# Moving input splits into attention and spreading a weight split over five tiles, at the seam of two stages of a fused kernel

## The chip, the cores and the metric

One Trainium2 chip, one core of it. The metric is device time of one execution in microseconds (us). The core has a matrix engine (PE, TensorE), a vector engine (DVE, VectorE), a scalar engine (ACT, ScalarE), GpSimd (POOL) and SP (SyncE), which here issues nearly all DMAs. Each engine works through its own queue in order and waits on semaphores that the others raise.

## The reference

Three layers in a row: pooled attention, a gated layer with a spatial product, a mixture of experts with one expert per token. What matters here is the first layer's end and the second layer:

```
q_pool = q.reshape(B, H, S // 2, 2, D).mean(axis=3)          # B 4, H 8, S 1152, D 64
attn = softmax(q_pool @ k^T / sqrt(D)); attn_out = attn @ v
x = attn_out.transpose(0, 2, 1, 3).reshape(B, 576, 512)
h = np.maximum(x @ w_in, 0.0); u, v = h[..., :512], h[..., 512:]
v_n = (v - mean(v)) / np.sqrt(var(v) + 1e-06)
v_s = np.einsum('ts,bsd->btd', w_spatial, v_n) + b_spatial[None, :, None]
x = (u * v_s) @ w_out                                         # then the experts
```

## The kernel before, in words

**Attention** (`attention`, L30 to L295) works on 16 pairs of heads, nine tiles each: 144 tiles g, t = g mod 9 within pair p. For a tile, PE makes scores (L82 to L98), DVE takes the largest (L105, L112), ACT the exponentials (L123, L125), PE transposes them (L137), DVE and ACT bring the transposes back (L155, L153), and PE multiplies by v (L203) into one accumulator `av`. Row sums are added and inverted on DVE (`sums`, L164, L165: instructions of 4 or 5 columns), turned by PE, stored to DRAM and loaded back broadcast over the partitions (`spread`, L188, L190, tile `rb`); DVE multiplies the accumulator by `rb` (L211, L213, `out`), and SP stores the result `xT` (L214). A table of times sets the order: `at(time, f)` puts a step at a place counted in tiles, and the sorted table is written out engine by engine; no scheduler moves anything. GpSimd sums and scales the next pair's q (`prep`, L71, L72), and 16 jobs round w_in into a high and a low part in the background (`weights_steps`).

All products of the later layers are made of a high part (rounded to the matrix engine's fast float32 form) and a low part (the rest): hi*hi + lo*hi + hi*lo. `split` (L365) makes the two: ACT rounds (L368), DVE or GpSimd subtracts (L372).

**The seam.** `Moe1.begin` (L393) loads batch 0's x when attention's last scores are issued, into the place where u's weights go later; `split_x` (L420) splits it on ACT, DVE and GpSimd beside the last products with v; `begin_x1` (L403) loads batch 1's x; `begin_u` (L407) loads u's weights after the last eviction. v's weights (`begin_v`, L387) come at tile 134.92, 2 MB.

**The gated layer** (`Moe1.rest`, L426) takes two batches at a time. Five v tiles come first (`v_tile`, L512): twelve matmuls, Relu on ACT (L522), statistics on DVE (L524 to L527), and one tile later `norm` (L529): a square root on ACT (L532), DVE's normalization (L533 to L537), vn's high part on DVE (L370) and its low part on GpSimd (L372). The fifth tile's rows go into `vta` and `vtb`, partly by SP's copies (L547). Between the v tiles stand batch 1's splits (L652 to L657). Then three u tiles (`u_tile`, L552), and the first spatial tile (`sp_tile`, L566), which needs vn, w_spatial's two parts (`wsh`, `wsl`) and `wt`, w_spatial's last tile with the bias. w_spatial (1.64 MB, L443) is loaded after the last store of x, and `w_rest` (L584) splits all five of its tiles together behind the second u tile. From there on the w_out conversion (`conv`, forty small steps on DVE and ACT) runs between the spatial tiles.

```
        def w_rest(norm):
            norm()
            for k in range(5):
                w_sp(k)
            bias()
```

## Time and profile before

| | us |
|---|---|
| runs shown | 1066.67, 1064.51, 1060.57; median 1064.51 |
| profiled execution, its own time | 1063.56 |
| its span, first to last instruction | 1061.7 |
| PE busy | 1008.2 (95%) |
| DVE busy | 748.7 (71%) |
| ACT busy | 595.3 (56%) |
| GpSimd busy | 225.5 (21%) |
| chain that ended last | PE 75%, DVE 10%, DMA 7%, issue 4%, ACT 2%, POOL 1% |

The times of the runs are of whole executions; the span leaves out 1.9 us around the instructions. Busy shares are means over stages with different limits: attention lasts to about 510 us of the span, the gated layer to about 750, the experts to the end. In a wait list the engine named first waited, the one behind the arrow ended the wait. In a chain of waits each piece was released by the one above it.

### The profile page before, as it was taken

The page shows a single profiled execution, that of the slowest core. Times are in us where ns is not written, and L with a number is a line of the kernel's source. Part 1 is how long each engine was busy: PE and PEld are TensorE (multiplying, and loading weights), DVE is VectorE, ACT ScalarE, POOL GpSimd, SP SyncE. Part 2 cuts the span into 40 slices and gives each one's busy share as a digit, 9 for nine tenths or more (in the row PEclk, how much of TensorE's full clock was granted, in tenths as well). Part 3 has the DMA queues.
Part 4 walks back from the last instruction along what each step waited for, and adds up shares of the span by engine and source line. Part 5 has one row for each costly group of instructions (what it writes and reads, how often), then busy time and mean ns, then how long its engine had stood idle before and what let it go on. Part 6 is the DMA issues. An engine that isn't in the chain of part 4 may idle for free.

```text
span 1061.7 us, 19763 instructions
## 1 busy us (share of the span) xinstructions
PE 1008.2 (95%) x7532; PEld 679.5 (64%) x7532; DVE 748.7 (71%) x1361; ACT 595.3 (56%) x1172; POOL 225.5 (21%) x189
## 2 busy tenths in 40 slices
PE   6899999999999999999879999999999999999997
PEld 3444444444544444444668988998777777777775
DVE  6787787878777787776498414232688787888884
ACT  4666666666666666666323322122277777777773
POOL 1111111111101111100355312231212321213111
PEclk9999999999999999999979999999999999999999
DMA  4444223443433343331512111001745142112840
GB/s 164 139 132 134 80 86 133 135 135 131 133 87 116 95 136 125 125 120 68 204 56 80 34 65 59 1 1 39 248 181 201 37 148 92 40 41 83 312 176 28
DMA packets 50495, 116.75 MB, mean 110 GB/s; under 512 B 8986, under 2 KB 21586, under 8 KB 48856
## 3 DMA queue, kind: packets, MB, share of 16 engines
q1 hardware_dynamic: 46672, 104.37, 29.0%
q0 software_dynamic: 3680, 11.02, 3.2%
q8 instruction: 62, 1.02, 0.4%
q14 instruction: 41, 0.34, 0.1%
q10 hardware_dynamic: 40, 0.01, 0.0%
HBM read 165.61 MB, written 19.47 MB: 174 GB/s over the span
## 4 chain that ended last, share of the span: by engine, by line
PE 75%; DVE 10%; DMA 7%; issue 4%; ACT 2%; POOL 1%; SPq 0%; POOLq 0%; DVEq 0%; ACTq 0%
PE ps_av L203 15%; PE ps_t L137 11%; PE ep_yp L1074 8%; PE ps_s L82 8%; PE ep_hp L1041 6%; DMA er_x<-x,tab_gi 4%; PE m_ps_v L626 4%; PE m_ps_u L574 4%; PE m_ps_u L560 3%; PE m_ps_v L519 3%; PE ep_hp L1034 3%; PE ps_r L95 3%; DVE aw_mx L105 2%; PE ps_s L85 2%; DMA ao_qr<-in_q 1%
## 5 line engine op out<-in xcount | busy, mean ns | idle before, releaser
L137 PEld LDWEIGHTS ps_t<-keep_ident,aw_e 64*128 64x128 f32 x2592 | 104.0, 140 | 193.1 <-DVE aw_et L155 130.3
L105 DVE TENSOR_REDUCE aw_mx<-ps_s 128x1 f32<-128x1024 f32 x144 | 174.7, 1213 | 8.3 <-ACT aw_e L125 2.5
L155 DVE COPY aw_et<-ps_t 128x640 f32<-128x640 f32 x144 | 118.5, 823 | 81.8 <-PE ps_t L137 81.5
L203 PE MATMUL ps_av<-aw_et,aw_v 128*64 128x320 f32 (+1 forms) x1152 | 168.9, 420 | 0.0
L125 ACT ACTIVATE aw_e<-ps_s,aw_mx 128x1024 f32<-128x1024 f32 x144 | 159.2, 1106 | 0.0
L137 PE MATMUL ps_t<-keep_ident,aw_e 64*128 64x64 f32 x2592 | 143.5, 235 | 15.8 <-DVE aw_et L155 12.0
L82 PE MATMUL ps_s<-ao_k,ao_q 64*128 64x512 f32 x512 | 141.7, 632 | 7.2 <-DMA ao_k<-in_k 6.0
L123 ACT ACTIVATE aw_e<-ps_r,aw_mx 128x128 f32<-128x128 f32 x144 | 53.0, 368 | 130.4 <-DVE aw_junk L112 130.4
L153 ACT ACTIVATE aw_et<-ps_t 128x512 f32<-128x512 f32 x144 | 86.0, 597 | 54.7 <-PE ps_t L137 53.4
L372 DVE TENSOR_TENSOR eb_w2l<-er_r,eb_w2h 128x1024 fp32r<-128x1024 f32 x88 | 103.5, 1217 | 4.2 <-ACT eb_w2h L368 4.1
L203 PEld LDWEIGHTS ps_av<-aw_et,aw_v 128*64 128x64 f32 x1152 | 72.0, 137 | 49.0 <-issue 4.1
L372 DVE TENSOR_TENSOR eb_w1l<-er_r,eb_w1h 128x1024 fp32r<-128x1024 f32 x66 | 78.7, 1221 | 33.6 <-ACT eb_w1h L368 33.6
L368 ACT ACTIVATE eb_w2h<-er_r 128x1024 fp32r<-128x1024 f32 x88 | 88.7, 1068 | 0.6 <-PE ep_yp L1074 0.3
L368 ACT ACTIVATE eb_w1h<-er_r 128x1024 fp32r<-128x1024 f32 x66 | 67.8, 1071 | 17.4 <-DMA er_r<-in_w 13.2
L372 POOL TENSOR_TENSOR bg_l<-bg_e,bg_h 128x256 fp32r<-128x256 f32 x16 | 11.6, 728 | 296.5 <-ACT bg_h L368 296.5
L1074 PE MATMUL ep_yp<-eb_w2h,ew_hth 128*128 128x512 f32 x176 | 71.2, 404 | 0.2 <-ACT ew_hth L368 0.2
L1074 PE MATMUL ep_yp<-eb_w2h,ew_htl 128*128 128x512 f32 x176 | 70.2, 399 | 0.2 <-DVE ew_htl L372 0.2
L1074 PE MATMUL ep_yp<-eb_w2l,ew_hth 128*128 128x512 f32 x176 | 69.1, 392 | 0.0
L1080 POOL DMA_INDIRECT out<-ew_y,tab_si x22 | 22.4, 1017 | 206.8 <-DVE ew_y L1079 183.2
L112 DVE TENSOR_SCALAR_CACHE_REDUCE aw_junk<-ps_r,aw_mx 128x128 f32<-128x128 f32 x144 | 49.9, 346 | 14.4
L71 POOL TENSOR_TENSOR ao_qr<-ao_qr 128x576 f32<-128x576 f32 x30 | 43.2, 1442 | 72.6 <-DMA ao_qr<-in_q 72.1
L95 PE MATMUL ps_r<-ao_k,ao_q 64*128 64x128 f32 x256 | 57.2, 304 | 0.0
(240 smaller groups left out, 1908.5 us busy)
## 6 DMA issues: line engine op xcount, KB each, us to landing
er_r<-in_w SPq DMA_DIRECT2D x45, 2048.0 KB
ao_qr<-in_q SPq DMA_DIRECT2D x32, 576.0 KB
ao_k<-in_k SPq DMA_DIRECT2D x32, 320.0 KB
aw_v<-in_v SPq DMA_DIRECT2D x16, 576.0 KB
xT<-aw_xo SPq DMA_DIRECT2D x16, 288.0 KB
bg_raw<-in_w_in SPq DMA_DIRECT2D x16, 256.0 KB
aw_rb<-rdram SPq DMA_DIRECT2D x64, 64.0 KB
er_r<-in_w SPq DMA_DIRECT2D x16, 256.0 KB
```

Source lines behind the costliest of these rows:

```text
L82: nc.tensor.matmul(d["s"][:, i, :], r["q", h][rows, 128 * n:128 * n + 128], r["k", h][rows, 0:512], start=True, stop=True)
L95: nc.tensor.matmul(d["r"][:, 0:128], r["q", h][rows, 128 * n:128 * n + 128], r["k", h][rows, 512:640], start=True, stop=True)
L105: nc.vector.tensor_reduce(out=m[:, 0:1], in_=d["s"], op=ALU.min, axis=AX.XY)
L125: nc.scalar.activation(out=e[:, 0:8, :].rearrange("p k c -> p (k c)"), in_=d["s"].rearrange("p i c -> p (i c)"), func=AF.Exp, bias=d["m"][ ...
L137: nc.tensor.transpose(t[:, i, 64 * (k - k0):64 * (k - k0) + 64], E[g]["e"][o, k, :], ident[o, o])
L153: nc.scalar.activation(out=o, in_=i, func=AF.Copy)
L155: nc.vector.tensor_copy(o, i)
L203: nc.tensor.matmul(box["t"][64 * h:64 * h + 64, 0:n], v[:, h, k, :], et[:, k, h, 0:n], start=k == 0, stop=k == 8)
L368: nc.scalar.activation(out=hi, in_=src, func=AF.Copy)
L372: (nc.gpsimd if eng_lo == "p" else nc.vector).tensor_tensor(out=lo, in0=src, in1=hi.bitcast(F32), op=ALU.subtract)
L1041: nc.tensor.matmul(pt[c], xT[xi][:, 128 * k:128 * k + 128], W1[wi][:, k, 512 * c:512 * c + 512], start=False, stop=todo[c] == 0)
L1074: nc.tensor.matmul(pt, hT[hi][:, c, 128 * o:128 * o + 128], W2[wi][:, f, :], start=f == 0 and (hi, wi) == (0, 0), stop=f == 7 and (hi, wi) ...
```

## The change

It concerns the seam. x of batches 0 and 1 is loaded at tile 82.3, when both are complete in DRAM, and split on GpSimd alone in eight steps (`begin_split`) at places of the table between tiles 86 and 140: one instruction rounds, one subtracts. The pool of q and k moves to the right side so that x's place on the left is free by then. u's weights are loaded at tile 137.92. In the last eviction DVE copies the accumulator to SBUF and multiplies from the copy. w_spatial's first four tiles are split one by one between the v tiles; the fifth stays where it was.

```diff
@@ -36,7 +36,7 @@
         early = ctx.enter_context(ExitStack())
-        opr = Pool(early.enter_context(tc.tile_pool(name="a_op", bufs=2)), "ao")
+        opr = Pool(early.enter_context(tc.tile_pool(name="a_op", bufs=2, side="right")), "ao")
         ps = Pool(ctx.enter_context(tc.tile_pool(name="a_ps", bufs=1, space=PSUM)), "ps")
@@ -207,6 +207,9 @@
                 xo, rb, t = P[p]["xo"], P[p]["rb", c], box["t"]
+                if p == NP - 1 and c:
+                    t = wrk([128, 320], F32, "av", bufs=1)
+                    nc.vector.tensor_copy(t, box["t"][:, 0:320])
                 m, e = (64, 0) if b % 2 else (0, 512)
@@ -275,11 +278,13 @@
             at(g + 1.11, evac)
-        at(NT - 1 + .3, lambda: (early.close(), hooks["S"]()))
+        at(NT - 1 + .3, early.close)
         at(NT - 10.4, lambda: [bg.pop(0)[1]() for _ in range(len(bg))])
-        at(NT - 9.08, hooks["raw"])
-        at(NT + 1.45, hooks["T"])
-        at(NT + 1.46, hooks["x1"])
+        at(82.3, hooks["x"])
+        for n, slot in enumerate((86, 95, 104, 113, 122, 125, 131, 140)):
+            at(slot + .21, hooks["split"], n)
+        at(NT - 9.08, hooks["v"])
+        at(NT - 6.08, hooks["u"])
         load_qk(0, 0)
@@ -292,7 +297,6 @@
         evac()
-        hooks["end"]()
@@ -395,14 +399,20 @@
         self.xx = [big([128, 4, 2 * SQ], F32R, f"x{i}") for i in "hl"]
-        self.x0 = [raw[h // 3][:, SQ * (h % 3):SQ * (h % 3) + SQ] for h in range(4)]
+        x0 = [raw[h // 3][:, SQ * (h % 3):SQ * (h % 3) + SQ] for h in range(4)]
         self.nc.sync.dma_start(raw[0][:, 0:3 * SQ], self.xT[0, :, 0:3, :])
         self.nc.sync.dma_start(raw[1][:, 0:SQ], self.xT[0, :, 3, :])
-        self.x1 = big([128, 4 * 640], F32, "wsh")[:, 0:4 * SQ].rearrange("p (h c) -> p h c", h=4)
-
-    def begin_x1(self):
-        for c in (slice(0, 64), slice(64, SQ)):
-            self.nc.sync.dma_start(self.x1[:, :, c], self.xT[1, :, :, c])
+        x1 = big([128, 4 * 640], F32, "wsh")[:, 0:4 * SQ].rearrange("p (h c) -> p h c", h=4)
+        self.nc.sync.dma_start(x1, self.xT[1])
+        self.raws = x0 + [x1[:, h, :] for h in range(4)]
+
+    def begin_split(self, n):
+
+        b, h = divmod(n, 4)
+        g, x, c = self.nc.gpsimd, self.raws[n], self.of(b, 0, SQ)
+        hi, lo = (self.xx[i][:, h, c] for i in range(2))
+        g.tensor_scalar(out=hi, in0=x, scalar1=1.0, scalar2=0.0, op0=ALU.mult, op1=ALU.add)
+        g.tensor_tensor(out=lo, in0=x, in1=hi.bitcast(F32), op=ALU.subtract)
@@ -432,6 +442,7 @@
         ps2 = self.ps2 = self.pool(self.right, "m_ps2", 3, space=PSUM)
+        wsh = self.big([128, 4, 640], F32R, "wsh")
         wsl = big([128, 4, 640], F32R, "wsl")
@@ -583,8 +594,7 @@
             norm()
-            for k in range(5):
-                w_sp(k)
+            w_sp(4)
             bias()
@@ -648,13 +658,9 @@
                     norm()
+                    if P == 0:
+                        w_sp(j - 1)
                 norm = n
-                if P == 0 and j == 1:
-                    c = of(1, 0, 64)
-                    split(nc, xx[0][:, :, c], xx[1][:, :, c], self.x1[:, :, 0:64], "a", "v")
-                if P == 0 and j == 2:
-                    split_x(1, [self.x1[:, h, 64:SQ] for h in range(4)], o=64)
-                    wsh = self.big([128, 4, 640], F32R, "wsh")
             norms = []
@@ -1209,8 +1215,8 @@
         bg = weights_steps(nc, Pool(bgp.enter_context(tc.tile_pool(name="bg", bufs=1, side="right")), "bg"), jobs, False)
-        hooks = {"raw": lambda: m1.begin_v(keep([128, 4096], F32R, "wv").rearrange("p (n k c) -> p n k c", n=2, k=4)),
-                 "S": m1.begin, "x1": m1.begin_x1, "T": lambda: m1.split_x(0, m1.x0), "end": m1.begin_u}
+        wv = keep([128, 4096], F32R, "wv").rearrange("p (n k c) -> p n k c", n=2, k=4)
+        hooks = {"x": m1.begin, "split": m1.begin_split, "v": lambda: m1.begin_v(wv), "u": m1.begin_u}
         attention(tc, nc, ap, cst, xT, bg, hooks)
```

The changed kernel's lines from L210 on are numbered higher: 3 more behind the copy (L212), 4 in `split` (L372, L376), 10 or 11 in `rest` (Relu L533, square root L543).

**ACT, over the first four square roots to the first u tiles.** `m_wrk_v` is a v tile's Relu, `m_wrk_mv` a square root, `m_a_xh` x's high part (its source `m_a_wsh` is batch 1's x), `m_a_wsh` as an output w_spatial's high part, `m_wrk_u` a u tile. Before:

```order
L368 ACTIVATE m_a_xh_6553<-m_a_wsh_6557 128x4x64
L522 ACTIVATE m_wrk_v_6785<-m_ps_v_6772 128x512
L532 ACTIVATE m_wrk_mv_6759<-m_wrk_mv_6759 128x1
L368 ACTIVATE m_a_xh_6553<-m_a_wsh_6557 128x512 x4
L522 ACTIVATE m_wrk_v_6822<-m_ps_v_6809 128x512
L532 ACTIVATE m_wrk_mv_6789<-m_wrk_mv_6789 128x1
L522 ACTIVATE m_wrk_v_6850<-m_ps_v_6837 128x512
L532 ACTIVATE m_wrk_mv_6826<-m_wrk_mv_6826 128x1
L564 ACTIVATE m_wrk_u_6890<-m_ps_u_6865 128x576
L564 ACTIVATE m_wrk_u_6917<-m_ps_u_6892 128x576
L532 ACTIVATE m_wrk_mv_6854<-m_wrk_mv_6854 128x1
L368 ACTIVATE m_a_wsh_6808<-m_r_gh_6703 128x640 x4
```

Now:

```order
L543 ACTIVATE m_wrk_mv_6749<-m_wrk_mv_6749 128x1
L372 ACTIVATE m_a_wsh_6708<-m_r_gh_6713 128x640
L533 ACTIVATE m_wrk_v_6795<-m_ps_v_6782 128x512
L543 ACTIVATE m_wrk_mv_6769<-m_wrk_mv_6769 128x1
L372 ACTIVATE m_a_wsh_6708<-m_r_gh_6713 128x640
L533 ACTIVATE m_wrk_v_6825<-m_ps_v_6812 128x512
L543 ACTIVATE m_wrk_mv_6799<-m_wrk_mv_6799 128x1
L372 ACTIVATE m_a_wsh_6708<-m_r_gh_6713 128x640
L533 ACTIVATE m_wrk_v_6855<-m_ps_v_6842 128x512
L543 ACTIVATE m_wrk_mv_6829<-m_wrk_mv_6829 128x1
L372 ACTIVATE m_a_wsh_6708<-m_r_gh_6713 128x640
L575 ACTIVATE m_wrk_u_6897<-m_ps_u_6872 128x576
```

x's rounding has left this stretch (and, ahead of it, batch 0's four), and one rounding of w_spatial stands behind each of the four square roots, the first ahead of the third Relu.

**SP, end of attention.** `aw_row` is the row of inverted sums on its way to DRAM, `aw_rb` the broadcast, `xT<-aw_xo` the last store of x, `m_a_wih` and `m_a_wil` from `xT` batch 0's x and from `wi_d` u's weights, `m_r_gh<-in_w_sp` w_spatial. Before, from the last pair's second row on:

```order
L180 DMA rdram<-aw_row_623_6626 5x128
L405 DMA m_a_wsh_6557<-xT 128x4x64
L405 DMA m_a_wsh_6557<-xT 128x4x512
L188 DMA aw_rb_624_6629<-rdram 64x2x128
L190 DMA aw_rb_624_6629<-rdram 64x64
L188 DMA aw_rb_624_6629<-rdram 64x2x128
L190 DMA aw_rb_624_6629<-rdram 64x64
L214 DMA xT<-aw_xo_6610 128x576
L410 DMA m_a_wih_6667<-wi_d 128x4x512
L410 DMA m_a_wil_6668<-wi_d 128x4x512
L442 DMA m_r_gh_6703<-in_b_sp 2x640 x2
L443 DMA m_r_gh_6703<-in_w_sp 128x5x640
```

Now:

```order
L180 DMA rdram<-aw_row_623_6647 5x128
L188 DMA aw_rb_624_6650<-rdram 64x2x128
L190 DMA aw_rb_624_6650<-rdram 64x64
L188 DMA aw_rb_624_6650<-rdram 64x2x128
L190 DMA aw_rb_624_6650<-rdram 64x64
L217 DMA xT<-aw_xo_6631 128x576
L453 DMA m_r_gh_6713<-in_b_sp 2x640 x2
L454 DMA m_r_gh_6713<-in_w_sp 128x5x640
```

Batch 1's x no longer stands between row and broadcast, nor u's weights between the store and w_spatial.

**GpSimd, pairs 10 to 12 in attention.** `ao_qr` and `ao_q` are the q preparation, `bg_l` the low part of a background job, `m_a_xh` and `m_a_xl` the new splits. Before:

```order
L372 TENSOR_TENSOR bg_l_4264<-bg_e_4066,bg_h_4263 128x256
L71 TENSOR_TENSOR ao_qr_67_4164<-ao_qr_67_4164 128x576
L72 TENSOR_SCALAR ao_q_71_4311<-ao_qr_67_4164 128x576
L71 TENSOR_TENSOR ao_qr_69_4216<-ao_qr_69_4216 128x576
L72 TENSOR_SCALAR ao_q_72_4352<-ao_qr_69_4216 128x576
L372 TENSOR_TENSOR bg_l_4635<-bg_e_4433,bg_h_4634 128x256
```

Now:

```order
L376 TENSOR_TENSOR bg_l_4278<-bg_e_4080,bg_h_4277 128x256
L71 TENSOR_TENSOR ao_qr_67_4178<-ao_qr_67_4178 128x576
L72 TENSOR_SCALAR ao_q_71_4325<-ao_qr_67_4178 128x576
L71 TENSOR_TENSOR ao_qr_69_4230<-ao_qr_69_4230 128x576
L72 TENSOR_SCALAR ao_q_72_4366<-ao_qr_69_4230 128x576
L414 TENSOR_SCALAR m_a_xh_3815<-m_a_wih_3813 128x576
L415 TENSOR_TENSOR m_a_xl_3816<-m_a_wih_3813,m_a_xh_3815 128x576
L376 TENSOR_TENSOR bg_l_4651<-bg_e_4449,bg_h_4650 128x256
```

A split of two instructions follows the second q preparation, ahead of the next background job.

## Rows read from the trace of the kernel before

**Rows 1.** PE time line, 510-552: start us, us, engine, line, op [idle before].
```profile
513.99 0.53 PE L519 MATMUL m_ps_v<-keep_wv,m_a_xh 128*128 128x512 f32 x1 [3.86 <-issue]
...
545.71 0.61 PE L574 MATMUL m_ps_u<-m_b_wsl,m_b_vnh 128*128 128x288 f32 x1 [6.41 <-DVE m_b_wsl L372]
...
549.96 0.61 PE L577 MATMUL m_ps_u<-m_b_wta,m_b_vta 128*128 128x288 f32 x1 [0.59 <-DVE m_b_wta L471]
```

**Rows 2.** Busy us by window: PE, PEld, DVE, ACT, POOL, clock, DMA, GB/s.
```profile
465.00:470.00 5.00, 5.00 (x60) 2.70 (x61) 3.54 (x8) 3.09 (x9) 0.00 (x0) 1.00 0.94 321
515.00:520.00 5.00, 5.00 (x17) 3.96 (x17) 0.69 (x1) 0.60 (x1) 0.00 (x0) 0.73 0.99 345
545.00:550.00 5.00, 3.42 (x12) 2.73 (x12) 4.90 (x6) 0.44 (x1) 2.01 (x1) 0.50 0.57 178
```

**Rows 3.** Chain that ended last, two stretches: start us, us, what.
```profile
513.99 7.36 PE m_ps_v L519 x24
...
644.91 13.60 PE m_ps_v L519 x60
658.52 9.54 PE m_ps_u L560 x72
```

**Rows 4.** DVE time line, 513-552.
```profile
513.20 0.42 DVE L211 TENSOR_TENSOR aw_xo<-ps_av,aw_rb 128x256 f32<-128x256 f32 x1 [4.56 <-DMA aw_rb<-rdram]
513.54 0.21 DVE L213 TENSOR_TENSOR aw_xo<-ps_av,aw_rb 128x64 f32<-128x64 f32 x1
...
525.09 0.42 DVE L372 TENSOR_TENSOR m_a_xl<-m_a_wsh,m_a_xh 128x256 fp32r<-128x256 f32 x1
...
528.04 2.39 DVE L372 TENSOR_TENSOR m_a_xl<-m_a_wsh,m_a_xh 128x512 fp32r<-128x512 f32 x2
...
531.55 1.30 DVE L534 SCALAR_TENSOR_TENSOR m_wrk_mv<-m_wrk_mv 128x1 f32<-128x1 f32 x1
...
543.61 4.13 DVE L372 TENSOR_TENSOR m_b_wsl<-m_r_gh,m_a_wsh 128x640 fp32r<-128x640 f32 x2
...
551.53 0.22 DVE L329 TENSOR_SCALAR m_wrk_xr<-m_wrk_o 128x256 int32<-128x256 int32 x1
```

**Rows 5.** Waits of PE, 552-594: us in total, times, longest us.
```profile
PE m_ps_v L519 <- ACT m_wrk_v L522: 0.9, 1, 0.9
PE m_ps_u L574 <- POOL m_b_vnl L372: 0.8, 1, 0.8
```

**Rows 6.** POOL, DVE and PE time lines, two places in attention.
```profile
104.17 1.45 POOL L71 TENSOR_TENSOR ao_qr<-ao_qr 128x576 f32<-128x576 f32 x1 [4.97 <-DMA ao_qr<-in_q]
...
104.28 1.36 DVE L164 SCALAR_TENSOR_TENSOR aw_rs<-aw_sum 128x5 f32<-128x5 f32 x1
...
168.16 0.16 DVE L164 SCALAR_TENSOR_TENSOR aw_rs<-aw_sum 128x5 f32<-128x5 f32 x1
...
102.67 1.08 PE L82 MATMUL ps_s<-ao_k,ao_q 64*128 64x512 f32 x4
...
111.98 1.08 PE L82 MATMUL ps_s<-ao_k,ao_q 64*128 64x512 f32 x4
...
166.55 1.08 PE L82 MATMUL ps_s<-ao_k,ao_q 64*128 64x512 f32 x4
...
173.15 1.08 PE L82 MATMUL ps_s<-ao_k,ao_q 64*128 64x512 f32 x4
```

**Rows 7.** SP time line, 513-518.
```profile
513.78 0.33 SPq L214 DMA_DIRECT2D xT<-aw_xo  x1
...
516.11 0.58 SPq L442 DMA_DIRECT2D m_r_gh<-in_b_sp  x2
516.74 0.39 SPq L443 DMA_DIRECT2D m_r_gh<-in_w_sp  x1
```

**Rows 8.** ACT time line, 530-560.
```profile
536.53 2.61 ACT L368 ACTIVATE m_a_wsh<-m_r_gh 128x640 fp32r<-128x640 f32 x4
...
548.31 0.44 ACT L333 ACTIVATE m_wrk_m<-m_wrk_o 128x256 f32<-128x256 f32 x1 [8.01 <-DMA m_wrk_o<-in_w_out]
```

## The prediction

> **What bounds the kernel now.** I read the 40 slices of the page first: the matrix engine (PE) is busy in every slice but the first, and the weak spot is in slices 19 to 21, where attention ends and the gated layer begins. So I took the list of waits from 505 to 600 us, then the time lines of all engines there, then the chain of work. Three rows tell the story on PE [rows 1]. It has nothing to do for 3.86 us ahead of the gated layer's first matmul at 513.99, for 6.41 us in the first spatial tile (until 545.71), and for 0.59 us in the same tile (until 549.96). After the first gap the granted clock is 0.73 over 515 to 520, after the second 0.50 over 545 to 550 [rows 2]; 1.00 is 2.4 GHz, 0.50 is 1.2 GHz. The first two v tiles took 7.36 us there, where five take 13.60 (2.72 each) at the full clock in the second round [rows 3]: 1.9 us lost.
>
> Who ends the gaps? The first is put down to "issue", but VectorE (DVE) waited 4.56 us for the broadcast reciprocals and began the last eviction only at 513.20 [rows 4]; the first matmul follows at once. The second and third are ended by DVE: it starts its two low parts of w_spatial at 543.61, and those, w_spatial's last tile and the bias end at 549.9. After that PE waits only twice until 594, 0.9 and 0.8 us [rows 5]. So a gain at 550 is kept only as far as DVE's and ScalarE's (ACT's) conversion of w_out, which starts at 551.53 [rows 4] and runs beside PE, comes forward too.
>
> **Part 1, the splits of x inside attention.** Added on GpSimd: 16 instructions, eight of them like the q sum of 1.45 us in [rows 6], the other eight with one input, bounded by the same: at most 23 us. GpSimd is 21% busy, so its own time is hidden by attention's PE work. Hidden there too are the loads of x (2.3 MB after tile 82) and of u's weights (2 MB after tile 138): v's weights, 2 MB, already arrive that way, with PE busy 5.00 of 5.00 us at 321 GB/s [rows 2]. Both now stand in SP's queue ahead of a broadcast of reciprocals, 2 MB being 6 to 7 us at that rate; their readers come some ten us later (three tiles), so I cost that at nothing, and at some 3 us once if it is late. Removed: x's splits of batch 0, which lay beside the last attention matmuls: nothing. The pool of q and k moving to the right: nothing.
>
> The danger is [rows 6]. A DVE instruction of five columns took 1.36 us, not 0.16, because a GpSimd sum had started 0.11 us earlier. Two tiles then took 111.98 - 102.67 = 9.31 us, against 173.15 - 166.55 = 6.60 undisturbed: 2.7 us. In GpSimd's order six of the new splits stand directly behind a q preparation and start when that ends; by the time line of those tiles that is early enough for DVE's next such instruction, two tiles on; I expect no collision, and keep 2.7 us each for the rivals. The Trainium skill (SBUF — State Buffer, section "SBUF: two separate sides") calls the pair of ports that DVE and GpSimd share an exclusive lock: whoever starts first keeps it for the whole instruction and the other blocks. The 1.36 us agree.
>
> **Part 2, the last eviction.** Attention's last matmul ends at 513.99 - 3.86 = 510.13. The new copy of 320 columns lies between the eviction of 256 columns (0.42 us, [rows 4]) and twice that: I take 0.46. With 0.05 ahead and the 0.24 that passed between the eviction's second part (to 513.75) and the matmul, PE starts at 510.9, 3.1 us sooner, and the clock should stay full, 1.9 us more. That is worth 5 us to PE, but by itself nothing at 550, where DVE decides.
>
> **Part 3, when w_spatial arrives.** SP loses two x transfers ahead of the broadcast, and their megabyte beside it, so I let the reciprocals land at 511.5, not 513.2 (bounds 510.7 and 513.2). The two multiplications end at 512.1, the store of x goes out, and the load of w_spatial waits for it: 513.78 to 516.11 is 2.3 us, and 0.6 more for the bias loads [rows 7]. So w_spatial is issued at 515.1, not 516.74. It is 1.64 MB and no longer shares with u's 2 MB: at 321 to 345 GB/s [rows 2] 4.8 to 5.1 us, and some 1.5 for start and end, an estimate: **W = 521.5**. Lower bound 520.5; upper bound 524, when it takes the 9 us that 3.7 MB need at 345.
>
> Here the change adds a wait. ACT's first rounding of w_spatial now stands between tile 1 and tile 2: the Relu of v tile 2, the square root behind it and DVE's statistics all wait for W. PE's fifth v tile needs the bank that this Relu empties: it starts at W + 0.65 + 0.6 = 522.8, where four tiles of 2.72 from 510.9 end at 521.8. PE loses 1 us, with DVE behind it anyway.
>
> **Part 4, DVE's way to the first spatial tile.** Before, DVE began its first split of batch 1's x at 525.09, with two statistics and one normalization done, and reached 549.9: 24.8 us without a real pause. By W those three are done in the new order as well, so the same work starts at W + 0.65 (one rounding of the 2.61 for four, [rows 8]) = 522.15, without
> - x's low parts, 0.42 + 2.39;
> - 1.1 of the 1.30 us that a one-column instruction at 531.55 took behind GpSimd's half of that split, [rows 4];
> - part of the 4.13 us of two low parts of w_spatial, made while GpSimd made its two. At the 0.42 us for 256 columns at 525.09, 640 want 1.0, two 2.0; now they are apart, but GpSimd has vn's low part beside them. I take off 1.2, between 0 and 2.1.
>
> 24.8 - 2.8 - 1.1 - 1.2 = 19.7, so the bias is ready at 541.9, not 549.9: 8.0 us sooner. PE gets there by 535 to 537 (five v tiles, three u tiles of 3.2, [rows 3]) and waits about 5 us; the clock will fall again. Bounds: W 520.5 and all of the 2.1 off give 540.0 (9.9 sooner); W 524 and neither deduction give 546.7 (3.2 sooner).
>
> By the skill's lock rule alone, each normalization of tiles 1 to 3 that meets GpSimd's vn or w_spatial part would block for its rest, up to 1.4 us three times, and the sum would be 4 us worse. By the rows such blocks are in the stretch already, as at 531.55, so I keep my sum; a rival takes the other end.
>
> **Part 5, what is late next.** The w_out loads are issued behind SP's copies of the last v rows, which wait for DVE at 543.61 before; ACT got w_out at 548.31 [rows 8], 4.7 us later. Now those rows are ready 2.2 us before the bias, at 539.7, so w_out is there at 544.4, while DVE is free at 541.9 + 1.6 = 543.5. The conversion starts 551.53 - 544.4 = 7.1 us sooner. PE comes 8.0 sooner, and some of ACT's work between the steps of the conversion waits for PE's u tiles, so I put the gain where the engines meet again between the two, at 7.5 us. From there to the end nothing else changes; it is a rigid shift.
>
> **Sum.** Attention 0, seam -7.5: 1063.56 - 7.5 = 1056.1 against the profiled execution's own time. The median of the runs, 1064.51, lies 0.95 above it, which gives 1057.0; I say **1056.5**.
>
> **Rivals.**
> 1. *The gain is half eaten* (24%): W near 524, because the load starts only when x's store has landed, and every meeting with GpSimd blocks as at 531.55. For it: 4.13 us for two parts that want 2.0. Against it: u's weights are out of the way. The bias comes 3.2 us sooner, w_out some 3: 1060 to 1061.
> 2. *Slower* (7%): the port in attention. If a split meets DVE's reciprocal sum, it costs 2.7 us; with the gain of 7.5, five of the eight must meet to make the kernel slower by 0.5%, and all eight give 1056.1 + 21.7 = 1078. For it: it happened at 104 us. Against it: the same q sums run in every head pair, and most meet nothing.
> 3. *PE is the bound after all* (6%): then all its idle time (3.9 + 6.4 + 0.9, less 0.8 that stays) and the half clock (1.9, and half of the 3.4 us that PE was busy in 545 to 550, [rows 2]) come back: 14 us, 1049.5. Against it: [rows 4], DVE has no idle time to give.
> 4. *The copy frees nothing*, if the first matmul still waits for the multiplications (they would end at 512.1): PE starts 1.5 us later, still ahead of DVE; the time is the forecast's. It has no chance of its own.
>
> **How the numbers follow.** The forecast, 1053 to 1059, has 62%; 1% is left for the unforeseen. About 0.5%, 5.3 us, is what a measurement of this kernel can tell from no change: below 1059.2 counts as faster, which is the forecast, rival 3 and little else, 68%; no change is rival 1, 25%; slower 7%. The range 1051.5 to 1063 takes in the forecast's bounds and rival 1, and leaves out the slower rival and most of rival 3.
>
> **What would show it.** Right: first matmul of the layer near 511 with the clock at 1.00; ACT waiting for w_spatial until 521 to 522 behind a square root; a PE gap of 4 to 6 us in the first spatial tile, ended by the bias near 542; conversion from about 544; attention's tiles as long as before. Wrong: DVE instructions of 1.3 us on five columns at tiles 86 to 140 (rival 2), the bias at 546 or later (rival 1), or no gap ahead of the first spatial tile (rival 3).

## The result, and the profile after

22 executions of each kernel, in turn: 1066.5 us before (median, 1060.6 to 1073.7), **1055.3 us** after (1050.4 to 1065.0), ratio 0.9902, 95% interval 0.9882 to 0.9923. The profiled execution of the changed kernel took 1053.34 us, span 1051.6, against 1063.56 before; the forecast was 1056.1 on that basis and 1056.5 for the runs. The time came within 1.2 us of the forecast for the runs. In part that is luck: behind attention's end the change gave 6.4 us where 7.5 were forecast, two steps that led there were wrong, and 2.8 us more are a difference of the two profiles in attention that the experiments put down to chance.

Three marks divide the spans: the end of attention's last matmul (a row's start and duration added), the start of the gated layer's sixteenth and last product of u with the spatial result on DVE (`m_wrk_g<-m_ps_u`; "the sixteenth product" below), and the end.

| us | before | after | difference |
|---|---|---|---|
| attention's last matmul ends | 510.14 | 507.34 | -2.80 |
| from there to the sixteenth product | 216.61 | 210.19 | -6.42 |
| from there to the end of the span | 334.95 | 334.07 | -0.88 |

PE's time line of the changed kernel, as in [rows 1]:

```profile
502.27 5.07 PE L203 MATMUL ps_av<-aw_et,aw_v 128*64 128x320 f32 x36
...
507.93 0.50 PE L530 MATMUL m_ps_v<-keep_wv,m_a_xh 128*128 128x512 f32 x1 [0.59 <-DVE aw_av L212]
...
519.42 0.50 PE L530 MATMUL m_ps_v<-keep_wv,m_a_xh 128*128 128x512 f32 x1 [0.32 <-ACT m_wrk_v L533]
...
537.54 0.37 PE L588 MATMUL m_ps_u<-m_b_wth,m_b_vta 128*128 128x288 f32 x1 [3.97 <-DMA m_b_vta<-m_wrk_xr]
...
540.20 0.58 PE L588 MATMUL m_ps_u<-m_b_wta,m_b_vta 128*128 128x288 f32 x1 [2.28 <-DVE m_b_wta L482]
...
568.75 0.50 PE L530 MATMUL m_ps_v<-keep_wv,m_a_xh 128*128 128x512 f32 x1 [1.67 <-ACT m_wrk_v L533]
```

v starts 0.59 us behind attention's last matmul, not 3.86. The gap in the first spatial tile is still there, 3.97 and 2.28 us. Busy time and clock by window, columns as in [rows 2]:

```profile
515.00:520.00 5.00, 4.68 (x22) 3.55 (x21) 2.96 (x10) 2.66 (x6) 1.29 (x1) 1.00 0.51 200
...
535.00:540.00 5.00, 0.37 (x1) 0.19 (x1) 4.84 (x6) 0.00 (x0) 2.14 (x2) 0.81 0.31 67
540.00:545.00 5.00, 4.80 (x20) 4.84 (x21) 4.17 (x13) 1.20 (x3) 0.27 (x1) 0.50 0.44 149
545.00:550.00 5.00, 5.00 (x40) 5.00 (x39) 4.41 (x8) 1.96 (x4) 2.86 (x3) 1.00 0.35 111
```

No half speed behind attention's end now (1.00, not 0.73), but again behind the gap (0.50, that is 1.2 GHz). Before, that stretch of half speed lasted longer, with PE busy in it for 3.42 us [rows 2] and then this:

```profile
550.00:555.00 5.00, 5.00 (x21) 5.00 (x22) 4.64 (x13) 0.76 (x2) 0.74 (x1) 0.50 0.10 36
```

PE's lists of waits between the first two marks add up to 12.9 us before and 9.6 after. Busy time times one minus the clock is an estimate of what half speed took: 1.4 + 1.7 + 2.5 = 5.6 us before (windows from 515, 545 and 550), 2.5 after (535 and 540). So on PE the 6.4 us sat in waits and in half speed, about half in each; what moved them, the experiments show.

DVE's time line, as in [rows 4]:

```profile
518.92 0.94 DVE L376 TENSOR_TENSOR m_b_wsl<-m_r_gh,m_a_wsh 128x640 fp32r<-128x640 f32 x1 [1.34 <-ACT m_a_wsh L372]
...
523.92 1.42 DVE L545 SCALAR_TENSOR_TENSOR m_wrk_mv<-m_wrk_mv 128x1 f32<-128x1 f32 x1
...
526.58 0.82 DVE L376 TENSOR_TENSOR m_b_wsl<-m_r_gh,m_a_wsh 128x640 fp32r<-128x640 f32 x1
...
530.15 1.27 DVE L545 SCALAR_TENSOR_TENSOR m_wrk_mv<-m_wrk_mv 128x1 f32<-128x1 f32 x1
531.46 1.50 DVE L546 SCALAR_TENSOR_TENSOR m_wrk_mv<-m_wrk_mv 128x1 f32<-128x1 f32 x1
...
539.17 0.88 DVE L482 SCALAR_TENSOR_TENSOR m_b_wta<-m_b_wta,keep_ident,m_r_gh 2x640 fp32r<-2x640 f32 x1
...
542.26 0.29 DVE L333 TENSOR_SCALAR m_wrk_xr<-m_wrk_o 128x256 int32<-128x256 int32 x1 [0.48 <-DMA m_wrk_o<-in_w_out]
...
717.53 0.76 DVE L590 SCALAR_TENSOR_TENSOR m_wrk_g<-m_ps_u,m_wrk_u 128x576 f32<-128x576 f32 x1 [5.03 <-PE m_ps_u L588]
```

The two low parts of w_spatial take 1.76 us together, not 4.13; three one-column instructions take 1.27 to 1.50 where their like take 0.16 to 0.22; the bias is ready at 540.05 and the conversion starts at 542.26. ACT's row, in which it waits for w_spatial:

```profile
518.15 0.74 ACT L372 ACTIVATE m_a_wsh<-m_r_gh 128x640 fp32r<-128x640 f32 x1 [2.33 <-DMA m_r_gh<-in_w_sp]
```

### The profile page after: what moved, and what is told of

Read it like the earlier page. It is cut to its first block, busy times and chain, and to the rows that moved or that the text cites. A ratio compares the mean times of both kernels' runs of the same rounds, so it can differ in the third digit from the quotient of the medians.

```text
span 1051.6 us, 19759 instructions
## 1 busy us (share of the span) xinstructions
PE 1001.9 (95%) x7532; PEld 675.1 (64%) x7532; DVE 743.1 (71%) x1357; ACT 590.5 (56%) x1163; POOL 239.4 (23%) x201
## 4 chain that ended last, share of the span: by engine, by line
PE 52%; issue 20%; DVE 12%; DMA 9%; POOL 3%; ACT 2%; SPq 1%; POOLq 0%; DVEq 0%; ACTq 0%
PE ps_av L203 14%; PE ps_t L137 10%; PE ps_s L82 8%; DMA er_x<-x,tab_gi 4%; PE m_ps_v L636 4%; PE m_ps_u L585 4%; PE m_ps_u L571 3%; PE ps_r L95 3%; PE m_ps_v L530 2%; POOL er_x L1007 2%; DVE aw_mx L105 2%; PE ps_s L85 2%; DMA ao_qr<-in_q 1%; DVE aw_et L155 1%; DMA er_r<-in_w 1%
## 5 line engine op out<-in xcount | busy, mean ns | idle before, releaser
L376 DVE TENSOR_TENSOR eb_w2l<-er_r,eb_w2h 128x1024 fp32r<-128x1024 f32 x88 | 103.5, 1218 | 4.6 <-ACT eb_w2h L372 4.5
L376 DVE TENSOR_TENSOR eb_w1l<-er_r,eb_w1h 128x1024 fp32r<-128x1024 f32 x66 | 78.8, 1221 | 34.5 <-ACT eb_w1h L372 34.5
L372 ACT ACTIVATE eb_w2h<-er_r 128x1024 fp32r<-128x1024 f32 x88 | 88.7, 1068 | 0.6 <-PE ep_yp L1080 0.3
L372 ACT ACTIVATE eb_w1h<-er_r 128x1024 fp32r<-128x1024 f32 x66 | 67.8, 1072 | 18.4 <-DMA er_r<-in_w 14.5
L376 POOL TENSOR_TENSOR bg_l<-bg_e,bg_h 128x256 fp32r<-128x256 f32 x16 | 11.6, 728 | 282.9 <-ACT bg_h L372 282.9
L71 POOL TENSOR_TENSOR ao_qr<-ao_qr 128x576 f32<-128x576 f32 x30 | 42.9, 1431 | 70.0 <-DMA ao_qr<-in_q 63.5
L1007 POOL DMA_INDIRECT er_x<-x,tab_gi x24 | 54.2, 2259 | 18.4 <-PE ep_xt L1028 7.3
```

The source lines that it names most:

```text
L372: nc.scalar.activation(out=hi, in_=src, func=AF.Copy)
L376: (nc.gpsimd if eng_lo == "p" else nc.vector).tensor_tensor(out=lo, in0=src, in1=hi.bitcast(F32), op=ALU.subtract)
L1007: nc.gpsimd.indirect_dma_start(out=X[s], out_offset=None, in_=x2, in_offset=bass.IndirectOffsetOnAxis(ap=route.gi[:, s:s + 1], axis=0), bo ...
```

## The experiments

Each edits the kernel before or the changed one. The five columns of a stage behind "that end" are in us; all but the last are counted from the end of attention's last matmul in the same profile. "Bias" is the end of `m_b_wta`, "conversion" the start of DVE's first step on w_out. Each ratio is to runs of the kernel before in the same series; those had medians of 1063.1 (before_copy, after_nocopy, after_together, after_u_late), 1065.4 (x_only, before_reduce, after_reduce, seam2) and 1064.7 us (after_again, seam3, seam3_reduce).

| kernel | that end | first v matmul | bias ready | conversion | 16th product | 16th product to end | median us (runs) | ratio to before, interval |
|---|---|---|---|---|---|---|---|---|
| before | 510.1 | 3.85 | 39.8 | 41.4 | 216.6 | 335.0 | 1066.5 (22) | |
| after | 507.3 | 0.59 | 32.7 | 34.9 | 210.2 | 334.1 | 1055.3 (22) | 0.9902 (0.9882 to 0.9923) |
| after_again | 510.1 | 0.59 | 32.7 | 34.8 | 210.0 | 333.7 | 1055.5 (10) | 0.9910 (0.9877 to 0.9943) |
| before_copy | 505.2 | 0.63 | 35.0 | 36.6 | 211.8 | 335.2 | 1063.1 (10) | 0.9969 (0.9930 to 1.0007) |
| x_only | 508.7 | 1.52 | 34.3 | 36.0 | 211.5 | 335.0 | 1057.6 (8) | 0.9913 (0.9884 to 0.9943) |
| after_nocopy | 505.1 | 1.31 | 33.4 | 35.3 | 210.6 | 333.8 | 1057.4 (10) | 0.9951 (0.9926 to 0.9976) |
| after_together | 509.0 | 0.59 | 33.4 | 35.0 | 210.2 | 333.6 | 1054.8 (6) | 0.9926 (0.9901 to 0.9952) |
| after_u_late | 506.6 | 0.59 | 36.7 | 38.7 | 214.0 | 340.4 | 1059.2 (10) | 0.9948 (0.9921 to 0.9976) |
| before_reduce | 507.9 | 3.82 | 39.7 | 41.3 | 218.1 | 341.7 | 1062.8 (12) | 0.9976 (0.9947 to 1.0006) |
| after_reduce | 510.8 | 0.59 | 32.7 | 34.8 | 210.1 | 334.5 | 1052.1 (6) | 0.9880 (0.9846 to 0.9914) |
| seam2 | 510.3 | 0.59 | 9.8 | 32.4 | 209.7 | 334.1 | 1054.0 (6) | 0.9882 (0.9847 to 0.9916) |
| seam3 | 505.6 | 0.59 | 10.1 | 29.8 | 206.2 | 333.7 | 1049.4 (6) | 0.9869 (0.9820 to 0.9917) |
| seam3_reduce | 507.2 | 0.59 | 8.8 | 28.4 | 206.2 | 333.4 | 1049.2 (6) | 0.9851 (0.9816 to 0.9886) |

The intervals are 4 to 10 us wide, so the table's times order the kernels only roughly; the stage columns separate them.

One row ties these columns together: the wait of PE in the second round of v tiles, at 568.75 above in the changed kernel and in the kernel before

```profile
577.97 0.50 PE L519 MATMUL m_ps_v<-keep_wv,m_a_xh 128*128 128x512 f32 x1 [0.88 <-ACT m_wrk_v L522]
```

The Relu that ends it stands on ACT behind steps of the conversion. PE goes on there 26.4 to 26.8 us after the conversion's start in all kernels but seam3 and seam3_reduce, and in nine kernels the sixteenth product follows 148.7 to 148.8 us later. So up to that wait PE's waits and its clock only decide how long it stands there (0.9 to 4.1 us); what moves the sixteenth product is the conversion's start. The exceptions behind the wait are before_reduce (150.3) and seam2 (150.8), where the clock fell to 0.50 after waits of 3.2 and 4.1 us, and the two seam3 kernels (149.1).

**The copy alone** (before_copy), the kernel before with

```diff
+                if p == NP - 1 and c:
+                    t = wrk([128, 320], F32, "av", bufs=1)
+                    nc.vector.tensor_copy(t, box["t"][:, 0:320])
```

> The kernel before, with nothing but the copy of the last accumulator to SBUF ahead of the last two multiplications. Theory (VectorE's chain behind w_spatial and x decides, not PE's idle time): the first v matmul follows attention's last matmul after some 0.6 us instead of 3.86 and the first two v tiles run at the full clock, yet the bias is ready 39.8 us after attention's last matmul, as before, within 1 us, and the time is that of the kernel before (ratio 1.00, within 0.003 either way). Rival (PE's idle time at the seam is what the change gave back): the 3.2 us and the 1.9 us of half clock come back, 3 to 5 us faster, ratio 0.995 to 0.997.

The theory fell. The bias came 4.8 us sooner (35.0, not 39.8), the conversion and the sixteenth product too. PE's and DVE's rows of this kernel:

```profile
505.85 0.47 PE L522 MATMUL m_ps_v<-keep_wv,m_a_xh 128*128 128x512 f32 x1 [0.64 <-issue]
...
536.02 0.61 PE L577 MATMUL m_ps_u<-m_b_wsl,m_b_vnh 128*128 128x288 f32 x1 [5.93 <-DVE m_b_wsl L375]
```

```profile
515.40 0.42 DVE L375 TENSOR_TENSOR m_a_xl<-m_a_wsh,m_a_xh 128x256 fp32r<-128x256 f32 x1
```

The first low part of batch 1's x, with which the prediction began its count of DVE's chain, starts 10.2 us behind attention's last matmul (505.22) here; in the kernel before it was 525.09 - 510.14 = 14.95 [rows 4]. From there to the bias both take 24.8 us. The reason stands in rows of the kernel before that the prediction did not use, ACT's and DVE's:

```profile
518.66 0.60 ACT L522 ACTIVATE m_wrk_v<-m_ps_v 128x512 f32<-128x512 f32 x1 [11.04 <-PE m_ps_v L519]
...
519.29 0.69 DVE L524 BATCH_NORM_STATS2 m_wrk_st<-m_wrk_v 128x6 f32<-128x512 f32 x1 [5.54 <-DMA m_a_wih<-wi_d]
```

DVE had stood idle for 5.54 us for the first v tile, and then 1.61 for the second. DVE's row names a load of u's weights as what ended the wait, but DVE starts 0.03 us after ACT's Relu of that tile ends (519.26), and the Relu waited for PE. The chain of 24.8 us is without a pause, but PE sets when it begins. With the copy PE is so early that something else holds the Relu, by its row the last store of x:

```profile
511.19 1.09 ACT L525 ACTIVATE m_wrk_v<-m_ps_v 128x512 f32<-128x512 f32 x2 [8.49 <-DMA xT<-aw_xo]
```

The runs (3.3 us faster in the ratio, interval from 7.4 faster to 0.7 slower; the medians are equal, 1063.1) allow either reading; the stage does not.

**The copy taken out** (after_nocopy): the same three lines removed from the changed kernel.

> The changed kernel without the copy: the last two multiplications read PSUM again. Theory: the first v matmul comes about 0.7 us later after attention's last matmul (two multiplications of 0.65 us in place of one copy of 0.49, if the broadcast has landed), the fifth v tile waits for w_spatial anyway, the bias stays 32.7 us behind attention's last matmul within 0.5 us, and the time is that of the changed kernel within 0.3%. Rival (the copy is a good part of the gain): 2 to 4 us slower than the changed kernel.

The first v matmul came 0.72 us later and the sixteenth product 0.37; the bias 0.67, a little more than allowed. So at the seam the same three lines are worth 4.8 us in the one kernel and 0.4 in the other: there the broadcast is what they avoid (it ended DVE's wait 3.06 us behind attention's last matmul, [rows 4]), here DVE's wait for it ends 0.56 us behind. The runs are not that clear: 0.9951 against 0.9902 and 0.9910 for the changed kernel is 4 to 5 us, as the rival had it or more, but these are ratios of different series, and the profiled execution took 1051.2.

**Only x's part** (x_only): the copy out, `at(NT - 6.08, hooks["u"])` moved behind the last `evac()`, and w_spatial's loop back in `w_rest`.

> Only the first part of the change: x of batches 0 and 1 loaded and split on GpSimd within attention, q and k on the right side; no copy, u's weights late, w_spatial split together as before. Theory A (what counts is when the matrix engine starts on v: either the copy or an unburdened broadcast queue gives that, so the parts overlap and don't add up): first v matmul some 1.3 us behind attention's last matmul, the bias 33 to 34.5 us behind it, the sixteenth product of the layer 210.3 to 211.5 us behind it (210.2 in the changed kernel, 216.6 before). Theory B (the prediction's sum: w_spatial's landing and its spreading decide): u's weights late cost their 3.8 us here too, 213.5 to 215 us.

Theory A held: 211.5 us, 5.1 of the 6.4, although u's weights are late and w_spatial is split in one piece. The copy alone gives 4.8, x's part alone 5.1, both and the rest 6.4: they don't add up, for both cure the same wait. How far, DVE's first cast of the normalized v shows, in the kernel before, before_copy and x_only:

```profile
524.75 0.43 DVE L370 CAST m_b_vnh<-m_wrk_vnf 128x512 fp32r<-128x512 f32 x1
...
515.06 0.43 DVE L373 CAST m_b_vnh<-m_wrk_vnf 128x512 fp32r<-128x512 f32 x1
...
519.39 0.43 DVE L371 CAST m_b_vnh<-m_wrk_vnf 128x512 fp32r<-128x512 f32 x1
```

It starts 14.6 us behind attention's last matmul before, 9.8 with the copy, 10.7 in x_only and 9.8 in the changed kernel. So the bias comes 4.8 us sooner with the copy by the earlier beginning alone; x_only's 5.4 are 3.9 of beginning and 1.6 of shorter chain, the change's 7.1 are 4.8 and 2.3.

**w_spatial in one piece** (after_together):

```diff
-            w_sp(4)
+            for k in range(5):
+                w_sp(k)
```

and without `w_sp(j - 1)` between the v tiles.

> The changed kernel with all five w_spatial tiles split together behind the second u tile, as before the change. Theory: VectorE loses the cover of its two low parts, which meet GpSimd's two (4.13 us for two in the kernel before, 0.94 + 0.82 in the changed one), less the 1.3 us for which it waited for the first rounded tile: the bias 1 to 2.5 us later than 32.7 us behind attention's last matmul, the time as much. Rival (the rounding ahead of the third Relu, which waits for the load, costs more than the spreading gives): the bias up to 1.5 us earlier. Rival (the spreading is the main part of the gain): 4 us or more later.

The bias came 0.7 us later, where the theory allowed 1 to 2.5, the conversion 0.1 later and the sixteenth product at the same 210.2: neither rival, and no effect on the time of the stage. The two low parts took their old 4.13 us again, while the third Relu no longer waited for the load:

```profile
536.08 4.13 DVE L376 TENSOR_TENSOR m_b_wsl<-m_r_gh,m_a_wsh 128x640 fp32r<-128x640 f32 x2
```

**u's weights late** (after_u_late): `at(NT - 6.08, hooks["u"])` removed, `hooks["u"]()` behind the last `evac()`.

> The changed kernel with u's weights (2 MB) loaded between attention's last store and w_spatial, as before the change. Theory: w_spatial lands 5 to 6 us later than 10.8 us behind attention's last matmul (2 MB at 345 to 410 GB/s), the third Relu and the fifth v tile stall as long, the bias comes 4 to 6 us later, and so does the end: 4 to 6 us slower than the changed kernel, about half of the change's gain lost. Rival (VectorE's work, not w_spatial's landing, sets the bias): at most 1.5 us later.

The theory's mechanism, a little smaller than it said: w_spatial 3.9 us later, not 5 to 6 (14.7 behind attention's end, not 10.8), PE's fifth v tile stalled, the bias 4.0 and the sixteenth product 3.8 later.

```profile
522.58 0.50 PE L530 MATMUL m_ps_v<-keep_wv,m_a_xh 128*128 128x512 f32 x1 [4.20 <-ACT m_wrk_v L533]
```

In x_only the same late weights cost at most 1.3 us (211.5 against 210.2 in after_together, which has the copy besides). Loading them early pays mainly because the tile-by-tile order hangs the v tiles on w_spatial's landing; the one part makes good what the other costs.

**Sums with one input** (before_reduce, after_reduce), for attention:

```diff
-            nc.vector.scalar_tensor_tensor(out=rs[:, 0:n], in0=s[:, 0:n, 0], scalar=1e-9, in1=s[:, 0:n, 1], op0=ALU.add, op1=ALU.add)
+            nc.vector.tensor_reduce(out=rs[:, 0:n], in_=s[:, 0:n], op=ALU.add, axis=AX.X)
```

> The kernel before, where the row sums are added by a reduction with one input in place of the instruction with two (1e-9 is no longer added to them). Theory (VectorE's instruction with two inputs in SBUF is what GpSimd's q preparation blocks): all 32 sums take under 0.3 us, none 0.5 or more (three took 1.36 before), attention's last matmul ends at 503 to 507 us (510.1 before), the seam behind it is 39.8 us to the bias and 216.6 to the sixteenth product as before, and the time is 2 to 6 us shorter with less spread. Rival (any small VectorE instruction is held up there): as many of 1.3 us as before, no change.

> The changed kernel with the same reduction. Theory: no sum over 0.3 us, attention's last matmul within 1.5 us of that of the kernel before with the reduction (attention's 2.8 us in the two profiles were blocked sums met by chance, not the splits' doing), and the two kernels with the reduction differ by the seam's 6.4 us, +-1.5. Rival (x's splits on GpSimd cost time in attention, or taking them from its end saves some): attention's ends differ by 2 us or more.

The slow sums were gone in both, and in seam3_reduce; in the ten other profiles one to three took 1.36 us each. All of these met the two-input instruction of the q preparation (L71); five more, in four of the profiles, took 0.57 to 0.63 beside its one-input instruction (L72). None met a split of x. The changed kernel's second one, GpSimd's row and DVE's:

```profile
409.35 1.64 POOL L71 TENSOR_TENSOR ao_qr<-ao_qr 128x576 f32<-128x576 f32 x1 [4.80 <-DMA ao_qr<-in_q]
```

```profile
409.65 1.36 DVE L164 SCALAR_TENSOR_TENSOR aw_rs<-aw_sum 128x5 f32<-128x5 f32 x1
```

But attention did not end sooner: 507.9 and 510.8 us. The first is above the 503 to 507 expected, and the 2.9 us between the two is more than the theory allowed, without a blocked sum in either. The seam missed as well: its sixteenth product came at 218.1 in before_reduce, not 216.6, with the bias and the conversion where they were, because of the wait of 3.2 us and the half clock named above. So the two kernels with the reduction differ by 8.0 us at the seam, 0.1 more than 6.4 +- 1.5. In attention, what differs is the clock. In after_reduce, windows as above, and the row of PE at the fall:

```profile
415.00:420.00 5.00, 4.97 (x30) 2.73 (x32) 3.18 (x5) 2.93 (x7) 3.63 (x4) 0.50 0.12 33
420.00:425.00 5.00, 4.99 (x46) 2.57 (x42) 2.97 (x6) 2.15 (x5) 0.00 (x0) 0.84 0.00 0
```

```profile
415.03 0.69 PE L137 MATMUL ps_t<-keep_ident,aw_e 64*128 64x64 f32 x8 [0.64 <-DVE aw_et L155]
```

The sum of 5 us x (1 - clock) over all windows of attention is an estimate of what the lowered clock took; with PE's idle time (the sum of its list of waits) it accounts for each profile's end:

| us | before | after | before_reduce | after_reduce | before_copy | after_nocopy |
|---|---|---|---|---|---|---|
| PE idle in attention | 28.0 | 26.3 | 26.9 | 26.3 | 27.2 | 25.6 |
| taken by the lowered clock | 5.1 | 3.4 | 3.4 | 6.9 | 0.0 | 1.7 |
| end less both | 477.0 | 477.6 | 477.6 | 477.6 | 478.0 | 477.8 |

**The changed kernel again** (after_again), unaltered.

> The changed kernel once more, unaltered. Theory (behind attention's last matmul the seam is the same in every execution; attention itself and the routing stage vary by chance, with blocked sums and dips of the clock): the sixteenth product 210.2 us behind attention's last matmul within 0.5 us, while attention's end lies anywhere from 505 to 511 us and equals 477.5 us plus PE's idle time plus the time that the lowered clock took, within 1 us. Rival (the seam varies from execution to execution too, so that one profile tells nothing of it): off by more than 1 us.

Both held: 210.0 us, and 510.1 = 27.7 + 5.1 + 477.3. Over all 13 profiles the last term lies between 477.0 and 478.7.

**A shorter chain on DVE** (seam2, seam3, seam3_reduce). In outline, on the changed kernel (the steps leave their old places):

```diff
-        at(NT - 1 + .3, early.close)
+        at(NT - 1 + .3, lambda: (early.close(), hooks["w"]()))
...
+    def begin_w(self):
+        self.mw = self.pool(self.left, "m_w", 1)
+        w = self.mw([128, 4096], F32, "vn")
...
+            if P == 0:
+                for k in range(4):
+                    w_sp(k)
             for j in (4, 0, 1, 2, 3) if P else range(5):
                 n = v_tile(a, j)
+                if P == 0 and j == 0:
+                    w_sp(4)
+                    bias()
```

and `load(0)`, `load(1)` of the conversion where its steps are made.

> The changed kernel with w_spatial and the bias loaded at attention's last scores (into the place of vn), all of w_spatial split and the bias made ahead of and behind the first v tile, and w_out's first two loads ahead of the copies of v's last rows. Theory (VectorE's chain is the bound at the first spatial tile, and the half clock and the late conversion follow from the gap): the chain ends 5 us sooner, PE waits at most 2 us there, the clock stays above 0.9, conversion starts some 28 to 31 us behind attention's last matmul (34.9), the sixteenth product comes 201 to 205 us behind it (210.2), 5 to 9 us faster than the changed kernel. Rival (the conversion of w_out on VectorE and ScalarE is the next bound): 207 us or more.

The bias was ready at 9.8 us, yet the sixteenth product came at 209.7: the rival. PE's gap in the first spatial tile fell to 1.2 us, but the conversion started only at 32.4, where 28 to 31 were expected, behind a small table that DVE casts first:

```profile
542.41 0.23 DVE L778 CAST tab_tri<-tab_table 128x128 bf16<-128x128 f32 x1 [3.61 <-DMA tab_table<-in_consts]
```

and PE then lost 4.1 us in the second round of v tiles, whose Relu stands behind the conversion. It went on there 2.6 us sooner behind attention's end than in the changed kernel (58.8, not 61.4), as the conversion started 2.5 sooner, and lost 2.1 of it again at half clock behind that wait:

```profile
569.13 0.79 PE L536 MATMUL m_ps_v<-keep_wv,m_a_xh 128*128 128x512 f32 x1 [4.10 <-ACT m_wrk_v L539]
```

```profile
570.00:575.00 5.00, 5.00 (x14) 3.94 (x14) 4.65 (x13) 1.26 (x3) 3.12 (x3) 0.50 0.35 105
```

So seam3 moves that table's load and casts (`at_leisure()`) behind the fourth v tile, and six casts to ACT:

```diff
+                if P == 0 and j == 3:
+                    at_leisure()
...
-                    split(nc, vn[0][:, j, :], vn[1][:, j, :], w, "v", "p")
+                    split(nc, vn[0][:, j, :], vn[1][:, j, :], w, "v" if b else "a", "p")
```

> Built on the changed kernel: w_spatial and the bias loaded at attention's last scores and split early, w_out's first loads ahead of the copies of v's last rows, and now also the small table whose landing held VectorE for 3.6 us loaded earlier, and the high parts of the first five v tiles rounded on ScalarE in place of VectorE (six instructions, some 2.8 us). Theory (from the first v tile to the last step of w_out's conversion VectorE is the bound, so each us taken off its chain comes off the end): conversion starts 26 to 29 us behind attention's last matmul, the sixteenth product comes 203 to 206 us behind it, 4 to 7 us less than in the changed kernel. Rival (PE's waits for ScalarE take over): 208 us or more.

> The same with the row sums added by the one-input reduction. Theory: behind attention's last matmul as the kernel without it, within 0.7 us; no sum of 0.5 us or more; attention's idle time 1 to 2 us less, which the chance dips of the clock cover in any one profile. Rival (the reduction is worth its 1.4 us per blocked sum in full): attention ends below 505 us.

206.2 us in both, 4.0 less than the changed kernel and 0.2 outside the range given; the conversion at 29.8 (26 to 29 expected) and 28.4. It came 5.1 and 6.5 us sooner than in the changed kernel, and the 1.4 us between the two changed nothing behind it: PE went on in the second round 57.1 us behind attention's end in both. So the conversion's start no longer decides there; what does isn't shown. seam3's list of PE's waits, 500 to 600 us (total, times, longest):

```profile
PE m_ps_v L536 <- ACT m_wrk_v L539: 4.3, 2, 3.1
PE m_ps_u L597 <- DMA m_b_vta<-m_wrk_xr: 2.1, 1, 2.1
```

The medians are 6 us below the changed kernel's of the same series (1049.4 and 1049.2 against 1055.5); the intervals of the ratios overlap. The reduction took 1.2 us of idle time out of attention (25.8, not 27.0), as expected, and no more.

## Why the prediction was right, and where it was not

**Part 1, splits in attention at nothing: right.** Each took 0.67 and 1.40 us on GpSimd, 16.6 us in all, where at most 23 were set. In ten profiles with them (eight with the two-input sums) no split met a sum, and attention's end less idle time and clock is 477.9 us on average with them, 477.5 without (three profiles). The rival of five or more collisions did not happen. The 2.8 us by which attention was shorter in the two profiles are idle time (1.7) and dips of the clock (1.7), less 0.6 in the rest; such differences also come in kernels with the same attention, whose end lay between 505.1 and 510.8.

**Part 2, the copy: PE's start right, its worth wrong.** PE started 0.59 us behind attention's last matmul (0.77 forecast) and the clock stayed at 1.00. The step that failed is "by itself nothing at 550, where DVE decides": alone it gives 4.8 of the 6.4 us. DVE decides the end of the chain, PE its beginning. The prediction read DVE's time line from 525.09 on, found no pause, and did not read the 5.54 us of idle time ahead of it. Rival 3 was turned down with the same thought ("DVE has no idle time to give"), which was wrong of DVE's time ahead of the chain; the rival did not come true because PE still waited 3.97 and 2.28 us in the first spatial tile.

**Part 3, w_spatial's landing: right in time, wrong in weight.** It landed 10.8 us behind attention's last matmul; 521.5 - 510.13 = 11.4 was forecast. Two errors in it partly cancel: SP issued the load 4.0 us behind that matmul (511.36), not 5.0, and from issue to landing it took 6.8 us, not 6.4. No run here shows the 1.5 us "for start and end" by themselves. The upper bound of 524 is a slip: 3.7 MB at 345 GB/s are 10.7 us, not 9, so it should have been 525.8. PE lost 0.3 us for the landing, not 1. But the order that makes DVE's chain hang on it is worth nothing (after_together), so this was a condition that the change makes and then meets.

**Part 4, the bias: 7.1 us sooner behind attention's last matmul, 8.0 forecast.** From the landing to the bias 540.05 - 518.15 = 21.9 us, not 541.9 - 521.5 = 20.4. The low parts gave back more than assumed (2.4 us, not 1.2). Against that stand the blocked one-column instructions. The sum took one of them out (1.1 us) and left a second in without naming it:

```profile
537.29 1.28 DVE L534 SCALAR_TENSOR_TENSOR m_wrk_mv<-m_wrk_mv 128x1 f32<-128x1 f32 x1
```

Now there are three, 1.42, 1.27 and 1.50 us for 0.22, 0.22 and 0.16, together 3.6 too long, where the sum kept only the 1.1 of the one at 537.29. So "such blocks are in the stretch already" held for one of the three; the other two cost 2.5 us that the sum put at nothing. That and the 1.2 us of the low parts make up 1.3 of the 1.5 us. GpSimd's rows beside the three:

```profile
523.77 1.56 POOL L376 TENSOR_TENSOR m_b_wsl<-m_r_gh,m_a_wsh 128x640 fp32r<-128x640 f32 x1
...
530.12 1.29 POOL L376 TENSOR_TENSOR m_b_vnl<-m_wrk_vnf,m_b_vnh 128x512 fp32r<-128x512 f32 x1 [1.57 <-DVE m_wrk_mv L544]
531.37 1.57 POOL L376 TENSOR_TENSOR m_b_wsl<-m_r_gh,m_a_wsh 128x640 fp32r<-128x640 f32 x1
```

Each DVE instruction starts 0.03 to 0.15 us after GpSimd's and ends 0.01 to 0.02 us after it. Two of the three partners are the low parts of w_spatial that the new order put between the v tiles. The Trainium skill (SBUF — State Buffer, section "SBUF: two separate sides") names the case: of a DVE instruction with two SBUF inputs and a GpSimd instruction that reads SBUF, the one that starts first holds the shared ports to its end and the other blocks. The trace agrees, and the one-input sums of before_reduce, after_reduce and seam3_reduce, none above 0.16 us, show no block. The prediction put three such blocks at 4 us by that rule and set it aside; the trace shows three.

**Part 5, the conversion: 6.5 us sooner, 7.1 forecast**, 34.9 behind attention's end. It decided, as said: the sixteenth product follows it (6.4), not the bias (7.1). Eleven profiles show it by PE's wait in the second round, and seam2 from the other side, where the bias came 22.9 us sooner than in the changed kernel and that wait ended only 2.6 sooner.

**The sum.** -6.4 in place of -7.5 at the seam, -2.8 by chance in attention, and 0.9 behind the layer, where the kernel before had a clock of 0.66 in one window of the routing (745 to 750) and the changed one 1.00. The runs' 10.4 us (interval 8.2 to 12.6) are more than the seam's 6.4 and those 0.9; the rest isn't settled. Attention isn't it by these profiles: without x's splits it ended at 507.8 us on average (three), with them at 508.1 (ten). Executions without a profile don't show where they spent their time. That 1056.5 lay so near 1055.3 owes something to the base too: the forecast started from 1064.51, the median of three runs, where 22 gave 1066.5.

## What to carry to other kernels

Where a chain on one engine runs without a pause, look at what starts it: an idle engine ahead of the chain names the part that a change can still move. Two cures of one wait don't add up, and a part may only pay for what another part of the same change has broken; undo each alone, and do each alone. Look for the row where the time of a stage is decided (here one wait of PE, a fixed 26.4 to 26.8 us behind the conversion's start): it tells which of several delays counts, and which are absorbed. Where runs scatter more than the parts are worth, compare stages from a common mark in the profiles, and check by a second profile of the same kernel that the stage repeats.

## What was not expected of the hardware

The clock of PE falls in some executions and not in others at the same place of the same instructions. In the routing stage of after_u_late it stood at 0.50 for some 17 us, though PE had been busy 4.94 of the 5 us before:

```profile
750.00:755.00 5.00, 4.94 (x47) 4.03 (x47) 4.90 (x12) 0.60 (x1) 1.49 (x1) 1.00 0.73 244
755.00:760.00 5.00, 5.00 (x60) 5.00 (x56) 2.37 (x10) 2.60 (x3) 3.52 (x3) 0.53 0.50 127
760.00:765.00 5.00, 5.00 (x26) 4.88 (x26) 0.90 (x1) 0.35 (x1) 0.64 (x1) 0.50 1.00 392
```

The same stage of the changed kernel kept 1.00. The stage behind the sixteenth product is 6.3 us longer there (340.4, not 334.1), and 341.7 us in before_reduce, which had such a stretch too (0.72, 0.50, 0.50 and 0.58 from 760 to 780): as much as the whole change gives at the seam. What sets it off isn't shown.
